# Joining the 64-token tails of two batches in the channel step of a fused attention and Wave-MLP kernel

## The chip, the cores and the metric

The kernel runs on one core of one Trainium2 chip. The metric is the device time of one execution in microseconds (us). A core has a matrix engine (TensorE, PE in the profile), a vector engine (VectorE, DVE), a scalar engine with function tables (ScalarE, ACT), a general engine (GpSimd, POOL) and a queue that issues transfers (SyncE, SP). Each takes its instructions in program order, and they wait for each other by semaphores.

## The reference, cut to what matters

There are 8 batches of 576 tokens, with 8 heads of 64 channels, all in float32. The first half is an attention with a pooled and a local part; its output `x` has 512 channels for each token. The second half mixes tokens and then channels:

```python
theta = x @ w_theta
zr, zi = x * cos(theta), x * sin(theta)
y = einsum('ts,bsd->btd', w_tok_r, zr) + einsum('ts,bsd->btd', w_tok_i, zi)
u = x + y
out = u + maximum(u @ w_ch, 0)
```

The change concerns `u` and the last line alone, and the order of the whole program.

## The kernel before

576 tokens are 4 chunks of 128 and a tail of 64. Everything is computed in steps of a few instructions, written as Python generators, one generator for each kind of step and all 8 batches one after the other. The string `ORDER` (line 80) has one letter for each step: `L` and `v` load q, k and v; `C` and `w` cast them (GpSimd mostly); `A` turns q and k so that channels lie on partitions (ScalarE copies the result, line 334; for batches 6 and 7 the turning itself is a DMA transpose, letter `q`, line 296); `Q`, `S` and `B` are pooled scores, band scores and pooled values; `N` and `V` are the two attention outputs (the third `N` step of a batch ends with a ScalarE copy, line 490); `T` transposes and adds them into `xT`; `H` makes the angles and their cosines and sines (lines 562 to 582); `Z` and `z` form z (lines 588 to 610); `X` mixes tokens (`mix`, lines 615 to 632); `u` turns `u` back with DMA transposes; `R` is the channel product (`channels`); `O` is the residual and the store (`store`). `l`, `c`, `h`, `g`, `W` are the weights, `D` is warm-up work for TensorE, `K` constants. A letter in the string takes the next step of its kind, so `X` letters 1 to 5 are batch 0. In the text "A7.2" means step 2 of the letter A for batch 7. A function `pin` ties each engine's instructions to just this order: the order in the string is the order on every engine and on the SP queue.

The accumulators have a fixed rotation too. Single-bank PSUM tiles come from `w1`, which goes round four tags, and two-bank tiles from `w2`, which goes round two. A step that takes a PSUM tile thus waits for whoever reads the tile of four (or two) allocations before.

For one batch the part that the change touches works so. `mix` makes `uT` (channels on partitions), 128 by 4 x 576: four chunks `dc` of 512 tokens (one `X` step each, nine matmuls of line 623) and the 64 tail tokens of all four in a fifth step (36 small matmuls, line 629). `u_turn` issues two DMA transposes on SP: `ur`, the 16 blocks of the main part (line 639), and `utr`, two blocks of the tail (line 641). `channels` has five steps: four chunks of 128 tokens, each of four matmuls of 512 columns (line 653), and the tail, for which the 64 tokens are put twice into the 128 columns of the array, each half giving 256 of the 512 channels: eight matmuls of 256 columns (line 661). `store` has five steps: one VectorE instruction each (`osb` = maximum(psr, 0) + ur, line 675), then one store of 128 tokens (line 681), and for the tail two stores of half the channels (line 684). `osb` has four buffers.

Of the kernel before, what the change touches and what calls it, by code (L numbers as in the profile page):

```python
# [10 lines left out]
BF16 = mybir.dt.bfloat16  # L11
AF = mybir.ActivationFunctionType
ALU = mybir.AluOpType
AX = mybir.AxisListType

P = 128
B = 8
H = 8
S = 576
# [22 lines left out]
HALF = 64  # L42
MAIN = 512
# [4 lines left out]
def kernel(  # L48
# [11 lines left out]
    nc = tc.nc  # L60
# [5 lines left out]
    moep = ctx.enter_context(tc.tile_pool(name="moep", bufs=2))  # L66
# [9 lines left out]
    def w1(name, dt=FP32):  # L76
        return ps1.tile([P, 512 if dt == FP32 else 1024], dt, tag="w1" + next(turn1), name=name)


    ORDER = (  # L80
        "LKLLLLLKKCLCCAvCCLvCDwvvvKLCAACwwwwLASCLSVQQCBlLLLLLVSlllllNvlCCCCNlvvvACNVCcScwcvTlTTccllcwAASlHVVH"
        "wwwDTTcAHZHZcHSZcccSDDhLLLzBcCSCWQDVWWLghLLLLCWCCvQvWWLNCNCCWWSWvvLvZNVVXwwwvAAvhwhTXTAALXSwSLLLLXQQ"
        "TBCCVgLggHCuLLVTvHNTVHHZNCCHCCCSwzZZZARRvvvSwOROALSXOLLAAXLLwSwwLvCCCCSCCCCRSNVOXVVXQVTTTAABwSXuTLLA"
        "vvwuvQRvvLLSTSHONNHVLLXuZZANHCLwHwwLVVHRQRRCCCCOzvLLLBOOCCSSTZTCvvRwOTLZSQHVHNVTXTAAXLLACACwCHHwCLCq"
        "LwwqNVHXSZNVXZZvvzSLLCCQCLqXVZLqQvRvwBvOVTVuTTLXTAwASSCHCCHCHNNXqvLwwTwuVXLVLAAHHXqSSZXRQROzONZSCCQC"
        "TCZBSVqROqvvvvZTSSROTVHVRHOTNNTXAAHVHHVwwwwwXAtAXSSzXXSSZZNZVuRuuRRROOQQtOOBRVRVttROtTTTOZOSTNXVRTuN"
        "RRxSSOOOHHVVXtttVHZHZZHNVzZXXttXuXTTXXHTHTTRxROOZHHRuROOHZRZZzOXXXXXXXRuRRRuuOORRuOOROROOORROO"
    )

    staged = {}  # L90
# [86 lines left out]
    for i in range(2):  # L177
        t = const.tile([P, 4, 5, KP], BF16, name=f"kdP{i}")
# [4 lines left out]
    for i in range(2):  # L183
        t = const.tile([P, 4, 5 * 120], BF16, name=f"kT{i}")
# [4 lines left out]
    for i in range(2):  # L189
        t = const.tile([P, NCH, H, 66], BF16, name=f"v_w{i}")  # L190
# [4 lines left out]
    for c in range(NCH):  # L195
        t = const.tile([P, DM], BF16, name=f"tmp{c}")
# [4 lines left out]
    for i in range(2):  # L201
        t = const.tile([P, 2, H, 66], BF16, name=f"vd{i}")
# [12 lines left out]
    wch = wpool.tile([P, 4, DM], BF16, name="wch")  # L215
# [305 lines left out]
    def parted(t):  # L521

        return (t[:, 0:4 * MAIN].rearrange("p (e t) -> p e t", e=4),
                t[:, 4 * MAIN:4 * S].rearrange("p (e t) -> p e t", e=4))
# [85 lines left out]
            yield  # L610


    uTs, urs = {}, {}

    def mix(b):

        (xA, xB), z = parted(xTs[b]), zs.pop(b)
        uT = uTs[b] = moep.tile([P, 4 * S], BF16, tag="uT", name=f"uT{b}")
        uA, uB = parted(uT)
        for dc in range(4):  # L620
            ps = w1(f"psu{dc}_{b}")
            for j in range(9):
                nc.tensor.matmul(out=ps, lhsT=z[:, j, P * dc:P * dc + P], rhs=WT[:, j, 0:MAIN], start=(j == 0), stop=(j == 8))  # L623
            nc.vector.tensor_tensor(out=uA[:, dc, :], in0=ps, in1=xA[:, dc, :], op=ALU.add)  # L624
            yield
        ps = w1(f"psut_{b}")[:, 0:4 * HALF].rearrange("p (e t) -> p e t", e=4)
        for dc in range(4):
            for j in range(9):
                nc.tensor.matmul(out=ps[:, dc, :], lhsT=z[:, j, P * dc:P * dc + P], rhs=WT[:, j, MAIN:S],  # L629
                                 start=(j == 0), stop=(j == 8))  # L630
        nc.vector.tensor_tensor(out=uB, in0=ps, in1=xB, op=ALU.add)
        yield

    def u_turn(b):

        ur = moep.tile([P, 16, P], BF16, tag="ur", name=f"ur{b}")
        utr = moep.tile([P, 2, P], BF16, tag="utr", name=f"utr{b}")
        urs[b] = ur, utr
        nc.sync.dma_start_transpose(out=ur, in_=uTs[b][:, 0:4 * MAIN])
        yield  # L640
        nc.sync.dma_start_transpose(out=utr, in_=uTs[b][:, 4 * MAIN:4 * S])
        yield

    rels = {}

    def channels(b):

        uA, uB = parted(uTs[b])
        for c in range(5):
            psr = rels[b, c] = w1(f"psr{c}_{b}")  # L650
            if c < 4:
                for dc in range(4):
                    nc.tensor.matmul(  # L653
                        out=psr, lhsT=uA[:, dc, P * c:P * c + P], rhs=wch[:, dc, :],
                        start=(dc == 0), stop=(dc == 3),
                    )
            else:

                for dc in range(4):
                    for hf in range(2):  # L660
                        nc.tensor.matmul(  # L661
                            out=psr[64 * hf:64 * hf + 64, 0:256], lhsT=uB[:, dc, :],
                            rhs=wch[:, dc, :].rearrange("p (j e d) -> p e j d", j=2, e=2)[:, hf],
                            start=(dc == 0), stop=(dc == 3),
                        )
            yield

    def store(b):

        ur, utr = urs.pop(b)  # L670
        for c in range(5):
            psr = rels.pop((b, c))
            osb = moep.tile([P, DM], FP32, tag="osb", bufs=4, name=f"osb{c}_{b}")
            n = 4 if c < 4 else 2
            nc.vector.scalar_tensor_tensor(  # L675
                out=osb[:, 0:P * n].rearrange("p (e d) -> p e d", d=P),
                in0=psr[:, 0:P * n].rearrange("p (e d) -> p e d", d=P), scalar=0.0,
                in1=ur[:, c:16:4, :] if c < 4 else utr, op0=ALU.max, op1=ALU.add,
            )
            if c < 4:  # L680
                nc.sync.dma_start(out=out[b, P * c:P * c + P, :], in_=osb)
            else:
                for hf in range(2):
                    nc.sync.dma_start(  # L684
                        out=out[b, 512:576, :].rearrange("t (j e d) -> e t j d", j=2, e=2)[hf],
                        in_=osb[64 * hf:64 * hf + 64, 0:2 * P].rearrange("p (j d) -> p j d", j=2),
                    )
            yield

    last = {}
# [13 lines left out]
    def batches(steps):  # L709
        for b in range(B):  # L710
            yield from steps(b)

    sequences = dict(L=batches(load), v=batches(load_v), C=batches(cast), w=batches(cast_v), A=batches(turns), B=batches(pooled_v), Q=batches(scores), S=batches(band_scores), N=batches(pooled_out), q=batches(turn_qk), t=batches(turn_x), x=batches(turn_z),
                     V=batches(outputs), T=batches(transposes), H=batches(phases), Z=batches(modulate),
                     K=constants(), z=batches(z_turn), u=batches(u_turn), X=batches(mix), R=batches(channels), O=batches(store),
                     l=weight_loads(), c=weight_casts(), h=channel_loads(), g=channel_casts(), W=weight_turns(), D=warm_up())
    pin()
# [35 lines left out]
```

## Time and profile before

| | before |
|---|---|
| time, median of 3 | 246.73 us (246.0 to 246.94) |
| profiled execution | span 247.0 us, 6608 instructions |
| TensorE busy | 224.8 us, 91% |
| VectorE busy | 184.6 us, 75% |
| ScalarE busy | 166.9 us, 68% |
| GpSimd busy | 160.9 us, 65% |
| tail of the channel product (line 661) | 64 matmuls, 5.0 us busy |
| tail of the residual (line 675, `utr`) | 8 instructions, 3.3 us |
| tail stores (line 684) | 16, of 64 KB each |
| `utr` transposes (line 641) | 8 |

The table is read together with where each piece stands. The busy time of TensorE is modelled for overlapping matmuls, so the start times of two successive instructions tell more about what one costs than its own duration does. An engine that is idle costs nothing as long as another one sets the pace.

### The profile page before, as it was taken

What the parts mean: (1) busy time and instruction counts of PE and PEld (TensorE: products, weight loads), DVE (VectorE), ACT (ScalarE), POOL (GpSimd) and SP (SyncE); (2) the same over time, 40 slices, a digit from 0 to 9 for tenths busy, and PEclk for the clock granted to TensorE, in tenths of its full rate; (3) what the DMA queues carried; (4) which work ended last, traced back from release to release, by engine and by line L of the source; (5) the groups of instructions that cost most, each with busy time, mean ns of one, the idle gap of its engine ahead of it and who ended that gap; (6) DMA issues with size and microseconds to landing.
All of it is one profiled execution on the core that took longest, in us unless ns stands there. A gap on an engine that the chain in (4) does not pass through costs nothing. (4 is left out here: it accounts for less than half of the span.)

```text
span 247.0 us, 6608 instructions
## 1 busy us (share of the span) xinstructions
PE 224.8 (91%) x2602; PEld 134.9 (55%) x2602; DVE 184.6 (75%) x345; ACT 166.9 (68%) x248; POOL 160.9 (65%) x223
## 2 busy tenths in 40 slices
PE   0778799999999999999999998999699999999990
PEld 0435465765566566656666555655455655455540
DVE  5274976679879898897989977997687776256462
ACT  3685799766998479988878999899924390250000
POOL 4467485997999999979759664996295942400000
PEclk9997999999999999999999999999989999999999
DMA  6999999999979997999999999599969594946496
GB/s 197 307 272 391 304 211 330 333 224 245 275 200 275 320 197 122 263 239 314 256 185 214 252 184 269 92 172 219 121 156 169 144 209 96 170 160 90 90 262 202
DMA packets 100511, 53.94 MB, mean 218 GB/s; under 512 B 83968, under 2 KB 86016, under 8 KB 100480
## 3 DMA queue, kind: packets, MB, share of 16 engines
q1 hardware_dynamic: 100480, 53.53, 93.3%
q8 instruction: 20, 0.33, 0.6%
q14 instruction: 11, 0.09, 0.2%
HBM read 33.59 MB, written 9.44 MB: 174 GB/s over the span
## 5 line engine op out<-in xcount | busy, mean ns | idle before, releaser
L623 PE MATMUL psu<-WT,z 128*128 128x512 bf16 x288 | 66.3, 379 | 0.5 <-ACT cs L568 0.5
L445 POOL TENSOR_SCALAR_AFFINE_SELECT pm<-pm 128x1024 bf16<-128x1024 bf16 (+1 forms) x35 | 36.6, 1045 | 20.0 <-ACT pm L438 20.0
L438 ACT ACTIVATE pm<-psS 128x1024 bf16<-128x1024 f32 (+1 forms) x40 | 37.7, 979 | 12.7 <-PE psS L430 11.9
L623 PEld LDWEIGHTS <-z 128*128 128x128 bf16 x288 | 26.8, 98 | 29.2 <-issue 0.8
L447 POOL TENSOR_SCALAR_AFFINE_SELECT pm<-pm 128x1024 bf16<-128x1024 bf16 (+1 forms) x35 | 36.6, 1045 | 2.4
L562 PE MATMUL psth<-wth,xT 128*128 128x512 bf16 x128 | 31.5, 379 | 0.1
L624 DVE TENSOR_TENSOR uT<-psu,xT 128x512 bf16<-128x512 f32 x32 | 21.8, 687 | 12.7 <-PE psu L623 12.6
L653 PE MATMUL psr<-wch,uT 128*128 128x512 bf16 x128 | 31.2, 383 | 0.0
L567 ACT ACTIVATE cs<-psth,pihc 128x512 bf16<-128x512 f32 x32 | 22.3, 697 | 11.8 <-PE psth L562 11.3
L131 POOL CAST v_w<-st_v 128x512 bf16<-128x512 f32 (+1 forms) x40 | 23.9, 614 | 9.2 <-DMA st_v<-in_v_dram 9.1
L511 DVE TENSOR_TENSOR tmp<-psloc,rl 120x512 bf16<-120x512 f32 (+2 forms) x40 | 27.6, 691 | 1.4
L342 DVE TENSOR_REDUCE qdT<-qT 128x288 bf16<-128x1152 bf16 x16 | 21.5, 1347 | 8.2 <-ACT qT L334 8.2
L675 DVE SCALAR_TENSOR_TENSOR osb<-psr,ur 128x512 f32<-128x512 f32 x32 | 21.6, 686 | 7.3 <-PE psr L653 6.7
L342 DVE TENSOR_REDUCE kdP<-kT 128x300 bf16<-128x1200 bf16 x16 | 22.3, 1397 | 5.8 <-ACT kT L334 5.8
L124 POOL CAST k_tm<-st_k 128x576 bf16<-128x576 f32 x32 | 21.5, 673 | 4.5 <-DMA st_k<-in_k_dram 4.3
L124 POOL CAST q_tm<-st_q 128x576 bf16<-128x576 f32 x28 | 18.7, 667 | 2.5 <-PE pstr L332 1.3
L334 ACT COPY qT<-pstr 128x576 bf16<-128x576 bf16 x24 | 14.2, 646 | 8.7 <-PE pstr L332 8.7
L545 DVE TENSOR_TENSOR xT<-xTps,xdT 128x480 bf16<-128x480 bf16 (+3 forms) x36 | 18.7, 548 | 0.9 <-PE xTps L541 0.7
L568 ACT ACTIVATE cs<-psth 128x512 bf16<-128x512 f32 x32 | 19.4, 606 | 0.0
L653 PEld LDWEIGHTS <-uT 128*128 128x128 bf16 x128 | 11.5, 99 | 12.2 <-issue 0.8
L430 PE MATMUL psS<-qT,kT 64*128 64x128 bf16 (+1 forms) x320 | 15.0, 220 | 3.1 <-ACT pm L438 2.2
L502 PEld LDWEIGHTS <-pm 128*128 128x128 bf16 (+1 forms) x320 | 14.9, 105 | 5.0 <-issue 0.7
(92 smaller groups left out, 390.2 us busy)
## 6 DMA issues: line engine op xcount, KB each, us to landing
st_q<-in_q_dram SPq DMA_DIRECT2D x32, 288.0 KB, 4.7
st_k<-in_k_dram SPq DMA_DIRECT2D x32, 288.0 KB, 5.0
st_v<-in_v_dram SPq DMA_DIRECT2D x32, 256.0 KB, 5.4
out_dram<-osb SPq DMA_DIRECT2D x32, 256.0 KB, 3.1
st_v<-in_v_dram SPq DMA_DIRECT2D x8, 192.0 KB, 4.8
tok<-in_moe_w_tok_r_dram SPq DMA_DIRECT2D x4, 288.0 KB, 7.6
tok<-in_moe_w_tok_i_dram SPq DMA_DIRECT2D x4, 288.0 KB, 4.2
th<-in_moe_w_theta_dram SPq DMA_DIRECT2D x2, 512.0 KB, 7.1
```

What stands on the lines that cost most here:

```text
L124: eng[i](out=dst[:, hh // 2, :, hh % 2, :], in_=staged.pop((b, f"{'qk'[i]}{hh}")).rearrange("p (r d) -> p r d", d=D))
L131: gp(out=v_ws[b % 2][0:KW[c], c, :, 0:D], in_=staged.pop((b, f"v{c}"))[0:KW[c], 0:DM].rearrange("p (h d) -> p h d", d=D))
L342: nc.vector.tensor_reduce(out=dst, in_=src, axis=AX.X, op=ALU.add)
L438: nc.scalar.activation(out=pv, in_=ps[0:kw].rearrange("p e (j w) -> p (e j) w", w=P)[:, :, 0:qn], func=AF.Exp, scale=SCL,)
L445: nc.gpsimd.affine_select(out=pv, in_=pv, compare_op=ALU.is_ge, fill=0.0, base=off, pattern=[[0, 8], [-1, qn]], channel_multiplier=1)
L447: nc.gpsimd.affine_select(out=pv, in_=pv, compare_op=ALU.is_ge, fill=0.0, base=6 - off, pattern=[[0, 8], [1, qn]], channel_multiplier=-1)
L511: nc.vector.tensor_tensor(out=tmp[0:cnt].rearrange("p (e j d) -> p e j d", e=2, j=4), in0=pv[0:cnt, :, :, 0:D], in1=rl[0:cnt].unsqueeze(3) ...
L562: nc.tensor.matmul(out=th, lhsT=xA[:, dc, P * c:P * c + P], rhs=wth[:, dc, :], start=(dc == 0), stop=(dc == 3),)
L567: nc.scalar.activation(out=cs[:, 0, :], in_=th, func=AF.Sin, bias=pihc, scale=1.0)
L623: nc.tensor.matmul(out=ps, lhsT=z[:, j, P * dc:P * dc + P], rhs=WT[:, j, 0:MAIN], start=(j == 0), stop=(j == 8))
L624: nc.vector.tensor_tensor(out=uA[:, dc, :], in0=ps, in1=xA[:, dc, :], op=ALU.add)
L653: nc.tensor.matmul(out=psr, lhsT=uA[:, dc, P * c:P * c + P], rhs=wch[:, dc, :], start=(dc == 0), stop=(dc == 3),)
```

## The change

The tails of batches 2i and 2i+1 become one chunk of 128 tokens. `u`'s tail gets a tile of its own, `uB`, for a pair of batches. The channel product, the residual and the store of the tails then happen once for a pair, in the steps of the odd batch, with the same form of instruction as any other chunk. The eight matmuls with the tail put twice into the array are gone, and so are the separate shapes in `store`. The purpose is fewer and more uniform instructions and transfers. Because even batches now have one `R`, `O` and `u` step fewer, the order string is a new one (682 letters for 694).

```diff
     def mix(b):
         (xA, xB), z = parted(xTs[b]), zs.pop(b)
-        uT = uTs[b] = moep.tile([P, 4 * S], BF16, tag="uT", name=f"uT{b}")
-        uA, uB = parted(uT)
+        uT = uTs[b] = moep.tile([P, 4 * MAIN], BF16, tag="uT", name=f"uT{b}")
+        uA = uT.rearrange("p (e t) -> p e t", e=4)
+        if b % 2 == 0:
+            uBs[b // 2] = moep.tile([P, 4, 2, HALF], BF16, tag="uB", name=f"uB{b // 2}")
+        uB = uBs[b // 2][:, :, b % 2, :]
...
     def u_turn(b):
-        nc.sync.dma_start_transpose(out=ur, in_=uTs[b][:, 0:4 * MAIN])
-        yield
-        nc.sync.dma_start_transpose(out=utr, in_=uTs[b][:, 4 * MAIN:4 * S])
-        yield
+        nc.sync.dma_start_transpose(out=ur, in_=uTs[b])
+        yield
+        if b % 2:
+            utr = utrs[b // 2] = moep.tile([P, 4, P], BF16, tag="utr", name=f"utr{b // 2}")
+            nc.sync.dma_start_transpose(out=utr, in_=uBs[b // 2].rearrange("p e i t -> p (e i t)"))
+            yield
...
     def channels(b):
-        for c in range(5):
+        for c in range(4 + b % 2):
             psr = rels[b, c] = w1(f"psr{c}_{b}")
-            if c < 4:
...
-            else:
-                for dc in range(4):
-                    for hf in range(2):
-                        nc.tensor.matmul(
-                            out=psr[64 * hf:64 * hf + 64, 0:256], lhsT=uB[:, dc, :],
-                            rhs=wch[:, dc, :].rearrange("p (j e d) -> p e j d", j=2, e=2)[:, hf],
-                            start=(dc == 0), stop=(dc == 3),
-                        )
+            for dc in range(4):
+                nc.tensor.matmul(
+                    out=psr, lhsT=uA[:, dc, P * c:P * c + P] if c < 4 else uBs[b // 2][:, dc],
+                    rhs=wch[:, dc, :], start=(dc == 0), stop=(dc == 3),
+                )
             yield
     def store(b):
-        for c in range(5):
+        for c in range(4 + b % 2):
...
             if c < 4:
                 nc.sync.dma_start(out=out[b, P * c:P * c + P, :], in_=osb)
             else:
-                for hf in range(2):
-                    nc.sync.dma_start(
-                        out=out[b, 512:576, :].rearrange("t (j e d) -> e t j d", j=2, e=2)[hf],
-                        in_=osb[64 * hf:64 * hf + 64, 0:2 * P].rearrange("p (j d) -> p j d", j=2),
-                    )
+                nc.sync.dma_start(out=out[b - 1:b + 1, 512:576, :], in_=osb)
             yield
```

Of the order, two stretches are spoken of later: from H5.0 to S7.1, and the end. In each the old order stands first.

```diff
-        H5.0 V5.4 R2.4 H5.1 O2.4 T5.3 N6.0 N6.1 T5.4 X4.0 A7.0 A7.1 H5.2 V6.0 H5.3 H5.4 V6.1
-        w7.0 w7.1 w7.2 w7.3 w7.4 X4.1 A7.2 t6.0 A7.3 X4.2 S6.3 S6.4 z5.0 X4.3 X4.4 S7.0 S7.1
+        H5.0 V5.4 H5.1 O2.3 v7.3 v7.4 N6.0 V6.0 T5.3 X4.0 T5.4 Z5.0 N6.1 A7.0 w7.2 A7.1 H5.2 H5.3 H5.4 V6.1
+        w7.3 w7.4 N6.2 A7.2 A7.3 X4.1 X4.2 S6.3 S6.4 X4.3 X4.4 S7.0 S7.1
...
-        X7.3 X7.4 R6.0 u6.0 R6.1 R6.2 R6.3 u6.1 u7.0 O6.0 O6.1 R6.4 R7.0 u7.1 O6.2 O6.3 R7.1 O6.4 R7.2 O7.0 O7.1 O7.2 R7.3 R7.4 O7.3 O7.4
+        X7.3 u6.0 u7.0 X7.4 R6.0 R6.1 R6.2 O6.0 O6.1 u7.1 R6.3 R7.0 O6.2 R7.1 R7.2 O6.3 O7.0 R7.3 R7.4 O7.1 O7.2 O7.3 O7.4
```

In the old order N6.2 came after S7.1.

More of the change, by code (lines that the diff above doesn't have):

```diff
@@ L80 @@
     ORDER = (
[L81 to L87, printed above, removed]
+        "LLLLLLKKCCCKKCLLvvvvCAvLDLLlCCLlllCwwAAASSSwwwVBCLvCQQVNNCAcCcCLlcNLLlllcTTCCvCcwASSHVVDTvvvccVTATww"
+        "AHllHZwwclHlZHSQDZzZDLLLLhcLLBSchQDccVWLLSWWWNCCCCCvNCCCWWSWWWvvvvvVVXwwvAANXAALwwXSwSTTLXLLQCQBggCL"
+        "LLTLHVVHTwVhThCNHHuwCCCZNHZAZZggCCSLLXzALLRSROONAvCvvLACCCXSwwSLwLLRSRCCCCvOVVvOXvvAVXAvvTBSSXQwLwww"
+        "VTTTATQSSHuNNZHXvCVwZANHHVVHLLLLRLLLQRRuzOOOCCCCCQBwTSSTTCCROvvSZHVVHZZNNXTLTAALLLXAAvLLCCHVHHCqwCwL"
+        "LqwwSXLvZNVXZSBVXzZvCCCLwLwCqLLQQqvvvTTTRuVVOXTAASSHXHTCNVXCCCLwCNwwAAHHqVHSNvXvvzXSLLQZZRqOZZSQRSBC"
+        "wCqCOVTROSwSTTqRVHVHOvvNVTXTZNAwAHHHVwwNAAXXSSXXSSZZZzRVuuuRRQQROOOBtStTOXVVtttRROTVTXTTxSSRHOOVVRRO"
+        "HtOttNNHHVZHNZZzZVXXXtTTXXtuTTXTHHHRHxRuOOROZROHRZZZzOXXXXXXuuXRRROOuRRORROORROOOO"
     )
@@ L610, in modulate @@
             yield
-    uTs, urs = {}, {}
+    uTs, uBs, urs, utrs = {}, {}, {}, {}
     def mix(b):
         (xA, xB), z = parted(xTs[b]), zs.pop(b)
-        uT = uTs[b] = moep.tile([P, 4 * S], BF16, tag="uT", name=f"uT{b}")
-        uA, uB = parted(uT)
+        uT = uTs[b] = moep.tile([P, 4 * MAIN], BF16, tag="uT", name=f"uT{b}")
[3 more added lines that the diff above has]
+        uB = uBs[b // 2][:, :, b % 2, :]
         for dc in range(4):
@@ L634, in u_turn @@
     def u_turn(b):
-        ur = moep.tile([P, 16, P], BF16, tag="ur", name=f"ur{b}")
-        utr = moep.tile([P, 2, P], BF16, tag="utr", name=f"utr{b}")
-        urs[b] = ur, utr
-        nc.sync.dma_start_transpose(out=ur, in_=uTs[b][:, 0:4 * MAIN])
+        ur = urs[b] = moep.tile([P, 16, P], BF16, tag="ur", name=f"ur{b}")
+        nc.sync.dma_start_transpose(out=ur, in_=uTs[b])
         yield
-        nc.sync.dma_start_transpose(out=utr, in_=uTs[b][:, 4 * MAIN:4 * S])
-        yield
+        if b % 2:
+            utr = utrs[b // 2] = moep.tile([P, 4, P], BF16, tag="utr", name=f"utr{b // 2}")
+            nc.sync.dma_start_transpose(out=utr, in_=uBs[b // 2].rearrange("p e i t -> p (e i t)"))
+            yield
@@ L644 @@
     rels = {}
     def channels(b):
-        uA, uB = parted(uTs[b])
-        for c in range(5):
+        uA = uTs[b].rearrange("p (e t) -> p e t", e=4)
+        for c in range(4 + b % 2):
             psr = rels[b, c] = w1(f"psr{c}_{b}")
-            if c < 4:
-                for dc in range(4):
-                    nc.tensor.matmul(
-                        out=psr, lhsT=uA[:, dc, P * c:P * c + P], rhs=wch[:, dc, :],
-                        start=(dc == 0), stop=(dc == 3),
-                    )
-            else:
-                for dc in range(4):
-                    for hf in range(2):
-                        nc.tensor.matmul(
-                            out=psr[64 * hf:64 * hf + 64, 0:256], lhsT=uB[:, dc, :],
-                            rhs=wch[:, dc, :].rearrange("p (j e d) -> p e j d", j=2, e=2)[:, hf],
-                            start=(dc == 0), stop=(dc == 3),
-                        )
+            for dc in range(4):
[3 more added lines that the diff above has]
+                )
@@ L666, in channels @@
             yield
     def store(b):
-        ur, utr = urs.pop(b)
-        for c in range(5):
+        ur = urs.pop(b)
+        for c in range(4 + b % 2):
             psr = rels.pop((b, c))
             osb = moep.tile([P, DM], FP32, tag="osb", bufs=4, name=f"osb{c}_{b}")
-            n = 4 if c < 4 else 2
             nc.vector.scalar_tensor_tensor(
-                out=osb[:, 0:P * n].rearrange("p (e d) -> p e d", d=P),
-                in0=psr[:, 0:P * n].rearrange("p (e d) -> p e d", d=P), scalar=0.0,
-                in1=ur[:, c:16:4, :] if c < 4 else utr, op0=ALU.max, op1=ALU.add,
+                out=osb.rearrange("p (e d) -> p e d", d=P),
+                in0=psr.rearrange("p (e d) -> p e d", d=P), scalar=0.0,
+                in1=ur[:, c:16:4, :] if c < 4 else utrs.pop(b // 2), op0=ALU.max, op1=ALU.add,
@@ L682, in store @@
             else:
-                for hf in range(2):
-                    nc.sync.dma_start(
-                        out=out[b, 512:576, :].rearrange("t (j e d) -> e t j d", j=2, e=2)[hf],
-                        in_=osb[64 * hf:64 * hf + 64, 0:2 * P].rearrange("p (j d) -> p j d", j=2),
-                    )
+                nc.sync.dma_start(out=out[b - 1:b + 1, 512:576, :], in_=osb)
             yield
```

## The prediction

> **What bounds the kernel now.** I read the busy shares first, then a table of busy time by stretch, then the timelines of TensorE, ScalarE and the SP queue where that table shows a change of limit.
>
> ```profile
> PE 224.8 (91%) x2602; PEld 134.9 (55%) x2602; DVE 184.6 (75%) x345; ACT 166.9 (68%) x248; POOL 160.9 (65%) x223
> ...
> 138.56:159.91 21.35, 19.96 (x265) 12.10 (x264) 17.46 (x32) 20.09 (x27) 15.64 (x21) 1.00 1.05 195
> 159.91:177.38 17.47, 15.52 (x176) 9.14 (x174) 14.29 (x25) 17.43 (x22) 10.85 (x14) 1.00 1.00 168
> 177.38:207.49 30.11, 29.84 (x332) 17.74 (x332) 22.97 (x45) 14.81 (x23) 20.06 (x22) 0.94 0.75 158
> 207.49:233.34 25.85, 25.85 (x207) 13.24 (x204) 12.13 (x20) 5.23 (x10) 4.81 (x6) 1.00 0.67 128
> 233.34:241.50 8.16, 8.12 (x48) 3.57 (x46) 5.52 (x9) 0.00 (x0) 0.00 (x0) 1.00 0.84 220
> 241.50:247.00 5.50, 0.00 (x0) 0.00 (x0) 1.20 (x3) 0.00 (x0) 0.00 (x0) 0.95 0.63 212
> ```
>
> After the length come TensorE, its weight loads, VectorE, ScalarE and GpSimd, then the granted clock. TensorE is the bound over all; but from 138.56 to 177.38 ScalarE is busy 37.5 of 38.8 us, and TensorE waits for it. From 177.38 to 241.5 TensorE is full. The last 5.5 us have no TensorE work: they are residuals and stores. What TensorE saves counts before 138 and after 177; what it saves between is lost in its wait.
>
> ```profile
> 172.63 2.36 ACT L334 COPY kT<-qk 128x576 bf16<-128x576 bf16 x2
> 175.01 1.28 ACT L438 ACT_TABLE_LOAD   x1
> 176.30 3.52 ACT L438 ACTIVATE pm<-psS 128x1024 bf16<-128x1024 f32 x4
> ```
>
> ```profile
> 174.25 1.21 PE L629 MATMUL psut<-WT,z 128*128 128x64 bf16 x36
> 177.38 0.40 PE L430 MATMUL psS<-qT,kT 64*128 64x128 bf16 x8 [1.92 <-ACT pm L438]
> 178.04 0.55 PE L430 MATMUL psS<-qT,kT 64*128 64x128 bf16 x8 [0.27 <-ACT pm L438]
> ```
>
> ```profile
> 174.90:178.30 3.40, 1.22 (x36) 1.04 (x31) 2.93 (x4) 3.37 (x5) 0.91 (x1) 0.98 0.62 136
> 178.30:181.70 3.40, 3.40 (x37) 2.62 (x33) 2.45 (x5) 2.16 (x3) 3.26 (x5) 0.52 0.83 154
> ```
>
> S7.0 needs the two-bank accumulator that the exponential of S6.3 reads, and that stands behind A7.3 and a table load. TensorE waits 1.92 and 0.27 us, and the next 3.4 us run at a clock of 0.52. With TensorE full there, that costs 3.4 x 0.48 = 1.6 us more.
>
> ```profile
> 220.23 0.63 PE L574 MATMUL pstt<-xT,wth 128*128 128x64 bf16 x16
> 220.79 0.63 PE L661 MATMUL psr<-wch,uT 128*64 128x256 bf16 x8
> 221.35 2.12 PE L623 MATMUL psu<-WT,z 128*128 128x512 bf16 x9
> ```
>
> The old tail's eight matmuls take 0.56 us from start to start; the sixteen before them take 0.47 in the chain of waits and start at 220.23, so 220.70 was due and they begin 0.1 us late. One old tail costs TensorE 0.66 us. A chunk of four 512-column matmuls takes 0.86 to 0.87 us (the 16 of 233.17 need 3.45).
>
> ```profile
> 240.84 0.63 PE L661 MATMUL psr<-wch,uT 128*64 128x256 bf16 x8
> 241.96 0.69 DVE L675 SCALAR_TENSOR_TENSOR osb<-psr,ur 128x512 f32<-128x512 f32 x1 [0.38 <-DMA out_dram<-osb]
> 242.79 0.42 DVE L675 SCALAR_TENSOR_TENSOR osb<-psr,utr 128x256 f32<-128x256 f32 x1
> 243.24 1.19 SPq L684 DMA_DIRECT2D out_dram<-osb  x2
> ```
>
> At the end VectorE waits for `osb` buffers, freed by stores; then two tail stores are issued, one after the other.
>
> [...] a store is 0.33 to 0.6 us on SP and 2 to 3.6 us to landing. [...]
>
> **The change part by part.**
>
> *Channel product.* A pair now costs 0.86 us where it cost 2 x 0.66 = 1.32. By place: R0.4 goes and R1.4 gets longer, before 138: -0.46. R2.4 stood inside the ScalarE-bound stretch (at 160.1), so its removal is absorbed; R3.4 comes after and costs +0.20. R4.4 and R5.4: -0.46. The last pair is counted with the end. Sum -0.72 us.
>
> *Residual, transposes, stores.* VectorE loses 2 x 0.42 and gains 0.69 for a pair: 0.15 us, hidden, as VectorE is under 60% after 207 and TensorE is the bound earlier. SP loses for a pair one transpose (1.19 us) and three of four tail store issues (0.59 each): 3.0 us, 12 in all. Before the end this is hidden: GpSimd waits for loads almost only before 40 us. For a tail transpose of four blocks I use z's row, also four blocks: 1.2 us on SP, 3.3 to landing, between utr's 2.8 and ur's 5.3. It hides behind nine chunks of product.
>
> *Waits added.* The tail of an even batch waits for the odd one: no engine stands still for it, as the steps are simply later in the order. The last utr transpose is issued after O6.1, and O6.2's store queues behind it on SP for 1.2 us, as it did before.
>
> *Order, ScalarE.* From H5.0 to S7.0 the ScalarE chain was table 1.28, H5.0 and H5.1 2.3, A7.0 and A7.1 4.5, the rest of H5 3.2, A7.2 and A7.3 4.5, table 1.28, one exponential 1.03. The new order puts N6.2 into it, with a copy of 0.65 us (line 490) that used to run at 180. TensorE reaches S7.1 0.65 us later: +0.65.
>
> *Order, accumulators.* Without R2.4, but with Z5.0 and N6.2 moved forward, the single-bank rotation shifts: X4.1 now needs the tile that H5.2's sines read. Counted from H5.0, TensorE is at X4.1 after 8.6 us (4 chunk products 3.5, X4.0 1.94, the rest small), and ScalarE ends H5.2 at about 10.0. So TensorE waits 1.4 us at X4.1 and 17.5 to 19.15, 1.65 us, at S7.0: the idle time is split and the later wait is shorter. The wait at X4.1 lies under the ScalarE chain and costs nothing by itself. If no window is then as empty as the 1.22 of 3.40 above, the half-rate window is not triggered where TensorE is full: -1.6 to -1.7 us.
>
> *End.* Let T0 be the end of X7.4 (233.33 before). Before, the product ended at T0+8.14 and the kernel at T0+13.67. Now nine chunks of 0.865 end at T0+7.8. O6.0 is at T0+0.9 and its store lands at about T0+5.2 (3.57 us, as in the chain); O7.0 takes its buffer and runs to about T0+6.5; its store lands at about T0+9.0; O7.4 takes that buffer, 9.0 to 9.7; one store instead of two (issue 0.5, landing 2.3 to 2.8) ends at about T0+12.7. That is -0.96 us, last pair included. If stores land 1 us sooner or later the end is T0+11.9 to 13.7.
>
> Sum: 246.73 - 0.72 + 0.65 - 0.96 - 1.7 = 244.0 us.
>
> **Rivals.**
>
> *The half-rate window stays.* All as above, but the wait at S7.0 still leaves a window too empty, or the one at X4.1 does. For it: 1.65 us plus a second short wait is about half a window. [...] 245.7 us, which is within 0.5%.
>
> *The new order opens waits in full stretches; slower.* From 42 to 138 TensorE has hardly a gap, and the new string changes all of that. z0.0 now stands before all of L2 on SP: its data come at about 39 us, so L2.0 goes at about 40.5 instead of 36.5, and lands at about 45 with C2.0 wanted near 46.5. T6.0 stands behind S7.2's two selections (2.2 us) on GpSimd, and H6.0 waits for it. Two such waits of 1.5 us with the half-rate window kept give 245.7 + 3.0 = 248.7, slower. Against it: TensorE's work, summed from its rows up to each of X1.0 to X6.0, differs by 1.3 us at most between the orders, but for X5.0, which has 4 us less ahead of it.
>
> *The front gets shorter.* H0.0 comes before A1.2 and A1.3; their loads go later. H0.0 could start near 26.5 instead of 29.8 us. But W needs all weight loads, which the transfers (share about 1 in the first 50 us) finish near 40 us in either order, so at most 1.5 us arrive at X0.0: 242.5.
>
> **How the numbers follow.** Forecast 244.0: 0.42. Window stays, 245.7: 0.28. Waits opened, 248.7: 0.17. Front shorter, 242.5: 0.13. Faster by over 0.5% is below 245.5: the forecast, the front, and a small part of the second case, less some of the forecast for small waits: 0.58. Slower, above 247.96: 0.17. The rest, 0.25, is the same. The range runs from 241.9 (front case, end 0.6 sooner) to 248.0, which leaves out most of the slower case.
>
> **What would show it.** Line 661 gone and 16 more matmuls of line 653; four utr transposes and four tail stores; the last product about 7.8 us after X7.4 and the end about 5 us after that. Near S7.0: the ScalarE chain with a copy of line 490 before A7.2, a TensorE wait of about 1.4 us at an X4 step and of 1.65 at S7.0, and no stretch near 0.5 of the clock after 170 us. The forecast is wrong if that stretch stands, or if TensorE starts X0.0 much later than 50.35 us or has new waits before 138 or after 180.

## The result, and the profile after

The changed kernel takes 255.95 us (254.36 to 256.55) where the kernel before takes 246.83; the ratio is 1.036, with an interval of 1.0301 to 1.0418. It is slower by 3.6%, where 244.0 us had been forecast. The profiled execution has a span of 254.8 us.

The page shows that TensorE has less to do, as meant, and a smaller share:

```profile
PE 221.1 (87%) x2517; PEld 134.6 (53%) x2554; DVE 186.6 (73%) x341; ACT 167.1 (66%) x248; POOL 161.7 (63%) x223
```

Read from the end. These are the last pieces of work in the changed kernel's timeline:

```profile
241.10 1.34 DVE L667 SCALAR_TENSOR_TENSOR osb<-psr,ur 128x512 f32<-128x512 f32 x2 [1.46 <-DMA out_dram<-osb]
241.98 0.75 PEld L655 LDWEIGHTS <-uB 128*128 128x128 bf16 x4
242.19 1.03 PE L655 MATMUL psr<-wch,uB 128*128 128x512 bf16 x4
243.30 1.40 DVE L667 SCALAR_TENSOR_TENSOR osb<-psr,ur 128x512 f32<-128x512 f32 x2 [0.86 <-PE psr L655]
244.69 0.69 DVE L667 SCALAR_TENSOR_TENSOR osb<-psr,utr 128x512 f32<-128x512 f32 x1
245.41 0.54 SPq L675 DMA_DIRECT2D out_dram<-osb  x1
```

The last store (line 675, 256 KB, the tails of batches 6 and 7) is issued at 245.41, and the span ends at 254.8. For 9.4 us no engine has work, and the program waits for its stores. In the kernel before, 3.8 us passed from 243.24 to the end, with two stores to issue. What the store does is seen in a table of stretches after it; the last two columns are the busy share of the 16 DMA engines and GB/s:

```profile
247.50:249.50 2.00, 0.00 (x0) 0.00 (x0) 0.00 (x0) 0.00 (x0) 0.00 (x0) 0.50 0.13 32
249.50:251.50 2.00, 0.00 (x0) 0.00 (x0) 0.00 (x0) 0.00 (x0) 0.00 (x0) 0.50 0.13 50
251.50:253.50 2.00, 0.00 (x0) 0.00 (x0) 0.00 (x0) 0.00 (x0) 0.00 (x0) 0.50 0.09 35
```

A share of 0.13 is what 2 of 16 engines give when they are busy all the time (0.125), and the rate is 32 to 50 GB/s. The packets of the trace say the same. The 128 packets of 2 KB of this store run from 246.58 to 252.93; two are under way at once for 5.8 us of this time, and never more than three. A group of two packets of 4 bytes (252.92 and 252.93) closes it, where sixteen (246.25 to 246.39) close the store of 128 tokens just before it. So this store is carried, by its share and its packets, by two engines.

The same store of batches 2 and 3 does harm in the middle. Three views of the changed kernel: its chain of waits, the VectorE timeline, the TensorE timeline.

```profile
191.80 8.00 DMA out_dram<-osb
```

```profile
195.36 0.68 DVE L667 SCALAR_TENSOR_TENSOR osb<-psr,ur 128x512 f32<-128x512 f32 x1
199.89 0.69 DVE L667 SCALAR_TENSOR_TENSOR osb<-psr,ur 128x512 f32<-128x512 f32 x1 [3.85 <-DMA out_dram<-osb]
```

```profile
201.56 0.47 PE L502 MATMUL psloc<-v_w,pm 128*128 128x65 bf16 x8 [2.34 <-DVE rd L476]
```

The store, issued at 191.80, takes 8.0 us to land and holds its `osb` buffer until then. The residual that takes this buffer next stands still for 3.85 us, and with it everything behind it on VectorE. TensorE needs one of these results and waits 2.34 us. Then its clock falls to 0.59 (the column before the DMA share):

```profile
199.00:202.40 3.40, 1.06 (x21) 0.88 (x20) 2.41 (x7) 1.69 (x4) 0.00 (x0) 0.91 0.98 284
202.40:205.80 3.40, 3.33 (x31) 2.21 (x30) 3.26 (x6) 1.28 (x3) 0.00 (x0) 0.59 0.95 227
```

The stretch before S7.0, on which the forecast turned, looks as it was drawn there. First the TensorE timeline, then ScalarE's, then stretches:

```profile
168.60 4.04 PE L626 MATMUL psu<-WT,z 128*128 128x512 bf16 x17 [1.43 <-ACT cs L568]
...
177.50 0.40 PE L430 MATMUL psS<-qT,kT 64*128 64x128 bf16 x8 [1.25 <-ACT pm L438]
178.17 0.40 PE L430 MATMUL psS<-qT,kT 64*128 64x128 bf16 x8 [0.27 <-ACT pm L438]
```

```profile
170.10 0.67 ACT L490 COPY xdT<-psxd 128x576 bf16<-128x576 bf16 x1
```

```profile
174.30:177.70 3.40, 2.15 (x49) 1.67 (x47) 2.58 (x5) 3.37 (x4) 0.18 (x1) 1.00 0.71 134
177.70:181.10 3.40, 3.08 (x43) 2.01 (x39) 3.10 (x8) 2.25 (x3) 3.26 (x4) 1.00 0.51 95
```

The wait is split over two places, the copy of N6.2 (line 490) stands in ScalarE's chain, and the clock stays at 1.00.

### The profile page after: what moved, and what is told of

It reads as the page before. It is cut to its first block, busy times and chain, and to the rows that moved or that the text cites. A ratio compares the mean times of both kernels' runs of the same rounds, so it can differ in the third digit from the quotient of the medians.

```text
span 254.8 us, 6438 instructions
## 1 busy us (share of the span) xinstructions
PE 221.1 (87%) x2517; PEld 134.6 (53%) x2554; DVE 186.6 (73%) x341; ACT 167.1 (66%) x248; POOL 161.7 (63%) x223
## 4 chain that ended last, share of the span: by engine, by line
PE 52%; ACT 14%; POOL 11%; DMA 8%; DVE 7%; issue 4%; SPq 1%; DVEq 0%; ACTq 0%; POOLq 0%
PE psu L626 19%; PE psr L655 7%; PE psth L562 5%; DMA out_dram<-osb 4%; POOL pm L445 4%; DMA st_q<-in_q_dram 4%; PE pstr L332 3%; POOL pm L447 3%; PE psloc L502 3%; ACT kT L334 3%; ACT pm L438 3%; PE psS L430 3%; DVE tmp L511 2%; DVE osb L667 2%; PE xTps L541 2%
## 5 line engine op out<-in xcount | busy, mean ns | idle before, releaser
L562 PE MATMUL psth<-wth,xT 128*128 128x512 bf16 x116 | 30.3, 379 | 0.9 <-issue 0.3
L655 PE MATMUL psr<-wch,uT 128*128 128x512 bf16 x118 | 30.3, 380 | 0.6 <-issue 0.2
L568 ACT ACTIVATE cs<-psth 128x512 bf16<-128x512 f32 x32 | 19.4, 606 | 0.0
L502 PE MATMUL psloc<-v_w,pm 128*128 128x65 bf16 (+1 forms) x320 | 16.5, 198 | 3.2 <-DVE rd L476 2.3
L605 DVE TENSOR_TENSOR z<-psxt,cs 128x1024 bf16<-128x1024 bf16 x24 | 15.8, 683 | 2.6 <-PE psxt L604 2.1
```

The costliest lines, as they stand in the source:

```text
L502: nc.tensor.matmul(out=pv[0:qn, h // 4, h % 4, :], lhsT=pms[b][c][0:kw, 4 * par + blk, 0:qn], rhs=v_w[0:kw, c, h, 0:65], start=(h % 4 == 0 ...
L562: nc.tensor.matmul(out=th, lhsT=xA[:, dc, P * c:P * c + P], rhs=wth[:, dc, :], start=(dc == 0), stop=(dc == 3),)
L655: nc.tensor.matmul(out=psr, lhsT=uA[:, dc, P * c:P * c + P] if c < 4 else uBs[b // 2][:, dc], rhs=wch[:, dc, :], start=(dc == 0), stop=(dc ...
```

## The experiments

Theory S: the view of `out` that the new store writes begins with a dimension of 2, so two engines carry it. Rival O: the new order. Rival Q: transfers that wait in the queue ahead of the store, or one large store as such. Each ratio is to the kernel before on the same chip.

**Two stores for a pair, new order.**

```diff
-                nc.sync.dma_start(out=out[b - 1:b + 1, 512:576, :], in_=osb)
+                for i in range(2):
+                    nc.sync.dma_start(out=out[b - 1 + i, 512:576, :], in_=osb[64 * i:64 * i + 64, :])
```

> The changed kernel, but the tail store of a pair goes as two stores of 64 tokens each. Theory S (the store): the changed kernel's one store, whose output view begins with a dimension of 2, is carried by few of the 16 DMA engines and so takes 8 to 9 us to land; it costs about 6 us at the end (the last store is issued at 245.4 and the span ends at 254.8, where 2.3 to 2.8 us to landing were due) and, by holding an osb buffer, 2.3 us of TensorE wait at 199 with a half-rate window after it of 1.7 us. Two stores land in 2 to 3 us each: 255.9 - 6 - 4 = 245.5 to 246.5 us. Rival O (the new order is at fault): 253 us or more, since the order is unchanged. Rival Q (transfers queue up: transposes before the store hold it): 254 to 256.

Measured: 246.48 us, ratio 0.9942 (0.9909 to 0.9976), span 246.0. The loss is gone, and the change is now a small gain. Rivals O and Q (in its queue form) fall.

**The old order with the change in it.** The order string is the old one without R, O and u steps for the tails of even batches.

> The change with the order of the kernel before, of which only the letters of the steps that are gone (tail steps of even batches) are struck out; the store as in the changed kernel. Theory S: the end is long as in the changed kernel, so at least 246.8 - 1.5 + 6 = 251.5 us; up to 256 if a slow store also holds an osb buffer in the middle. Rival O: 245.5 to 246.5. Rival Q: the late transposes are at the same places as before, so about 247.

Measured: 255.79 us, ratio 1.0304 (1.0249 to 1.0358). Theory S allowed up to 256 if the store also does harm in the middle. It does, but by another way than the `osb` buffer. The order has a transpose (line 304) right behind the store of batches 2 and 3 on SP. GpSimd waits 3.70 us for that transpose, its masks come late, and TensorE waits 1.97 us for them. In the next run, with the same order and two stores, TensorE has no such wait from 180 us on. In the GpSimd and TensorE timelines:

```profile
198.67 0.95 POOL L545 TENSOR_TENSOR xT<-xt,xdT 128x112 bf16<-128x112 bf16 x2 [3.70 <-DMA xt<-tmp]
```

```profile
201.89 0.43 PE L502 MATMUL psloc<-v_w,pm 128*128 128x65 bf16 x8 [1.97 <-POOL pm L447]
```

Rival O expected 246.

**The old order, two stores.** Both edits above.

> As the run with the old order, and the pair's tail store in two. This is the change without its new order and without its one store. Theory S and rival O: 245 to 246.5 us. What it differs from the two-store run with the new order is what the new order is worth: by my working the front gains 1.5 us (X0.0 at 48.85 instead of 50.35) and loses it again in waits on ScalarE before 178, so no more than 1 us either way.

Measured: 247.39 us, ratio 0.999 (0.9956 to 1.0024). The change in the code alone, with quick stores, is worth nothing that can be measured in the old order. The new order with quick stores gives 0.9942, thus about 0.5% from the order, though the two intervals overlap a little.

**One store, the tokens of two batches interleaved.** The bytes and the number of stores are those of the changed kernel; the first dimension of the view is 64 instead of 2. The transpose and the matmul read `uB` in its new order; these two lines are left out here.

```diff
-            uBs[b // 2] = moep.tile([P, 4, 2, HALF], BF16, tag="uB", name=f"uB{b // 2}")
-        uB = uBs[b // 2][:, :, b % 2, :]
+            uBs[b // 2] = moep.tile([P, 4, HALF, 2], BF16, tag="uB", name=f"uB{b // 2}")
+        uB = uBs[b // 2][:, :, :, b % 2]
...
-                nc.sync.dma_start(out=out[b - 1:b + 1, 512:576, :], in_=osb)
+                nc.sync.dma_start(out=out[b - 1:b + 1, 512:576, :].rearrange("i t d -> t i d"), in_=osb)
```

> The changed kernel with one store for a pair as it has, of the same 256 KB, but the two batches' tail tokens interleaved on the partitions (token 0 of both, token 1 of both), so that the output view begins with a dimension of 64 instead of 2. Nothing is left out. Theory S in the form that the first dimension sets how many engines carry the store: the store lands in 2 to 3 us and the time is that of the two-store run within 0.7 us, 245 to 246.5. If merging into one 256 KB store is itself slow (rival Q, or one large store to two distant places): 254 to 256 as in the changed kernel.

Measured: 246.15 us, ratio 0.9911 (0.9887 to 0.9936), span 244.7. The end of its SP timeline, and a stretch after the last issue:

```profile
240.68 0.57 SPq L675 DMA_DIRECT2D out_dram<-osb  x1
```

```profile
241.50:242.50 1.00, 0.00 (x0) 0.00 (x0) 0.00 (x0) 0.00 (x0) 0.00 (x0) 1.00 0.64 240
```

The share is 0.64 at 240 GB/s, and 4.0 us pass from issue to the end of the span instead of 9.4. The size of the store and its two distant targets are not what was slow.

**Two stores for a pair, split by channels.** Each still begins with a dimension of 2.

```diff
-                nc.sync.dma_start(out=out[b - 1:b + 1, 512:576, :], in_=osb)
+                for i in range(2):
+                    nc.sync.dma_start(out=out[b - 1:b + 1, 512:576, 256 * i:256 * i + 256], in_=osb[:, 256 * i:256 * i + 256])
```

> The changed kernel with two stores for a pair as in the two-store run, but split by channels: each has both batches' 64 tokens and 256 channels, so the output view of each still begins with a dimension of 2. Theory S, in which that first dimension sets the number of engines: still slow, two stores of 128 packets of 1 KB on the same two engines: 253 to 258 us. Rival (what helped was having two smaller stores): 245.5 to 247.

Measured: 254.85 us, ratio 1.029 (1.0227 to 1.0352). Half the size and twice the number do not help; two stretches after the last issue show about the same share as in the changed kernel (0.13):

```profile
247.00:249.00 2.00, 0.00 (x0) 0.00 (x0) 0.00 (x0) 0.00 (x0) 0.00 (x0) 0.50 0.14 42
249.00:251.00 2.00, 0.00 (x0) 0.00 (x0) 0.00 (x0) 0.00 (x0) 0.00 (x0) 0.50 0.14 48
```

**Only the last pair's store in two.** The edit of the first experiment under `if b == 7`.

> The changed kernel; only the store of the last pair (batches 6 and 7) goes in two, the other three pairs keep the one store. Theory S: the end shrinks by about 6 us, the wait at 199 stays: 255.9 - 6 = 249.5 to 250.5 us. A rival in which only the end matters: 246 to 247. A rival in which the middle matters more: 252 or more.

Measured: 250.97 us, ratio 1.0136 (1.0059 to 1.0214). By the ratios 2.2%, about 5.5 us, came from the end, near the 6 expected. The wait in the middle stands, in its TensorE timeline:

```profile
200.91 0.41 PE L502 MATMUL psloc<-v_w,pm 128*128 128x65 bf16 x8 [2.62 <-DVE rd L476]
```

**Only the store of batches 2 and 3 in two.** The same under `if b == 3`.

> The changed kernel; only the store of batches 2 and 3 (issued at 191.8 us in the changed kernel) goes in two. Theory S: the VectorE wait of 3.85 us for an osb buffer at 196 to 199.9 and the TensorE wait of 2.34 us go, and the half-rate window that followed goes in most executions: 251.5 to 253.5 us, the end as long as before (8 to 9 us after the last store). Rival (that wait came from the 5.2 us transpose ahead on the same queue): no change, 255 to 256.

Measured: 252.3 us, ratio 1.0199 (1.0127 to 1.0271). The stretch from 180 to 210 us has no wait and a full clock (third column from the right):

```profile
180.00:210.00 30.00, 29.63 (x288) 16.16 (x292) 21.23 (x42) 11.85 (x19) 21.47 (x25) 1.00 0.81 170
```

With the last pair split alone, TensorE was busy 26.84 us of this stretch, at a clock of 0.94. The rival that this run was to test blamed a transpose of 5.2 us that follows the store on SP. That transpose is itself an effect of the store: with this one store in two, it takes 1.84 us. The changed kernel's line stands first.

```profile
194.46 5.21 SPq L312 DMA_TRANSPOSE xr<-xT  x1
```

```profile
194.06 1.84 SPq L312 DMA_TRANSPOSE xr<-xT  x1
```

By ratios the middle is worth 1.036 - 1.020 = 1.6% and the end 2.2%, each uncertain by about 0.9%; all four stores together are worth 4.2%.

**N6.2 back behind S7.1, in the interleaved kernel.** One letter of the order string is moved.

```diff
-        V6.1 w7.3 w7.4 N6.2 A7.2 A7.3 X4.1 X4.2 S6.3 S6.4 X4.3 X4.4 S7.0 S7.1
+        V6.1 w7.3 w7.4 A7.2 A7.3 X4.1 X4.2 S6.3 S6.4 X4.3 X4.4 S7.0 S7.1 N6.2
```

> The kernel with interleaved tails (246.15 us, ratio 0.991), with one letter moved: N6.2, which the new order put ahead of A7.2, goes back behind S7.1. It tests the two steps of the prediction on the stretch before S7.0. Theory C (clock): without N6.2 ahead, X4.1 takes an accumulator that is free, so TensorE reaches S7.0 early and waits once, about 1.9 to 2.2 us, and a half-rate window after it comes back in most executions: S7.1 about 0.65 us earlier, but 1.6 us lost after it, so about 1 us slower, 246.8 to 247.5. Rival L (the ScalarE chain alone matters): 0.65 us faster, 245.3 to 245.7.

Measured: 249.18 us, ratio 1.0056 (1.0022 to 1.009). The interleaved kernel, on other chips, had 0.9911 and in a later measurement 0.9952, so this is 1.0 to 1.5% slower. The direction is that of theory C. The size, 2.5 to 3.6 us, is larger than its 1 us, and what makes up the rest stays open. In its TensorE timeline the wait is one again, and the row of granted clock on its page has a dip after it, in the slice that begins at 179.0 us (the 30th digit):

```profile
177.40 0.40 PE L430 MATMUL psS<-qT,kT 64*128 64x128 bf16 x8 [1.92 <-ACT pm L438]
```

```profile
PEclk9997999999999999999999999999979999999996
```

S7.1 did not come earlier, as it was expected to. But this execution was already late before the letter that was moved: ScalarE's chain, which begins with the table load ahead of H5.0, began 0.73 us later. The table load and S7.1, in the profile of the interleaved kernel and then here:

```profile
159.20 1.28 ACT L567 ACT_TABLE_LOAD   x1 [0.76 <-issue]
...
177.84 0.40 PE L430 MATMUL psS<-qT,kT 64*128 64x128 bf16 x8 [0.27 <-ACT pm L438]
```

```profile
159.93 1.28 ACT L567 ACT_TABLE_LOAD   x1 [0.76 <-issue]
...
178.07 0.47 PE L430 MATMUL psS<-qT,kT 64*128 64x128 bf16 x8 [0.27 <-ACT pm L438]
```

From the one to the other it is 18.64 us in the interleaved kernel and 18.14 here. The chain is 0.50 us shorter without N6.2, near the 0.65 of the expectation.

**N6.2 ahead of A7.2, in the kernel before.** Again one letter.

```diff
-        V6.1 w7.0 w7.1 w7.2 w7.3 w7.4 X4.1 A7.2 t6.0 A7.3 X4.2 S6.3 S6.4 z5.0 X4.3 X4.4 S7.0 S7.1
+        V6.1 N6.2 w7.0 w7.1 w7.2 w7.3 w7.4 X4.1 A7.2 t6.0 A7.3 X4.2 S6.3 S6.4 z5.0 X4.3 X4.4 S7.0 S7.1
```

> The kernel before, with one letter moved: N6.2 from behind S7.1 to behind V6.1, ahead of A7.2, as in the new order. Theory C: ScalarE's chain gets 0.65 us longer, but the idle time of TensorE is split between X4.1 (1.4 us) and S7.0 (1 to 1.3), and the half-rate window after S7.1 goes away: 0.65 - 1.65 = 1 us faster than before, ratio 0.995 to 0.997. Rival L: 0.65 us slower, ratio 1.002 to 1.004. Rival F (the window falls by chance): no difference on the mean, mean granted clocks spread alike in both.

Measured: 246.79 us where the kernel before had 247.59; ratio 0.9968 (0.9951 to 0.9986), as theory C had it. From its TensorE timeline and stretches:

```profile
168.49 4.05 PE L623 MATMUL psu<-WT,z 128*128 128x512 bf16 x17 [0.95 <-ACT cs L568]
...
177.39 0.40 PE L430 MATMUL psS<-qT,kT 64*128 64x128 bf16 x8 [1.26 <-ACT pm L438]
```

```profile
174.90:178.30 3.40, 1.88 (x53) 1.66 (x51) 2.93 (x4) 3.37 (x5) 0.89 (x1) 1.00 0.46 101
178.30:181.70 3.40, 3.35 (x36) 2.02 (x32) 2.84 (x6) 1.53 (x2) 3.26 (x5) 1.00 0.83 154
```

S7.0 starts where it did in the kernel before (177.38), but the clock after it is 1.00 and not 0.52. Rival F (chance) falls too. None of the 22 executions of this kernel had a mean granted clock below 0.987, where 12 of 36 of the kernel before did; and all 15 executions with N6.2 moved back in the interleaved kernel were at 0.987 or below. The profiled executions of the two kernels agree: from 177 to 184 us the kernel before, with N6.2 behind S7.1, has a mean clock of 0.76, and the changed kernel, with N6.2 ahead of A7.2, has 1.00.

**Six `osb` buffers, and the interleaved kernel once more beside it.**

```diff
-            osb = moep.tile([P, DM], FP32, tag="osb", bufs=4, name=f"osb{c}_{b}")
+            osb = moep.tile([P, DM], FP32, tag="osb", bufs=6, name=f"osb{c}_{b}")
```

> The kernel with interleaved tails, and six osb buffers instead of four. It tests the step on the end: there O7.0 to O7.3 wait for osb buffers (1.23 and 0.86 us) that come free only when a store has landed. If that chain sets the last residual, O7.4 ends about 0.8 us after the last matmul group instead of 1.9, and the kernel is 0.8 to 1.2 us faster than the interleaved kernel of the same call. Rival (the store queue or the transposes set it: ur of batch 7 lands late): no change within 0.3 us.

> The kernel with interleaved tails once more, on the same chip as the run with six osb buffers, for the comparison and a narrower interval: 0.989 to 0.994 of the kernel before, as it was.

Measured: six buffers 246.07 us, ratio 0.9924 (0.9901 to 0.9947); four buffers 246.77 us, 0.9952 (0.9931 to 0.9973). On VectorE at the end of the run with six:

```profile
236.82 2.04 DVE L667 SCALAR_TENSOR_TENSOR osb<-psr,ur 128x512 f32<-128x512 f32 x3 [0.55 <-DMA ur<-uT]
239.03 0.69 DVE L667 SCALAR_TENSOR_TENSOR osb<-psr,ur 128x512 f32<-128x512 f32 x1 [0.17 <-PE psr L655]
239.90 0.69 DVE L667 SCALAR_TENSOR_TENSOR osb<-psr,utr 128x512 f32<-128x512 f32 x1 [0.17 <-PE psr L655]
```

The waits for buffers are gone; what is left is one for `ur` of batch 7 and then TensorE's own pace. The last residual ends at 240.59, 0.9 us after the last matmul group (238.83 + 0.86), where it was 2.05 us in the run beside it (242.81 against 239.90 + 0.86). The gain of 0.7 us on the median is a little below the expected 0.8 to 1.2, and the two intervals overlap; the shorter wait in the trace is clearer than the time. This version, new order, interleaved tails and six buffers, is faster than both kernels.

## Why the prediction was wrong

**The step that failed** is the last term of *End*: "one store instead of two (issue 0.5, landing 2.3 to 2.8)". The landing was taken from stores of another shape. Issue and landing together measured 9.4 us to the end of the span, and 8.0 us for the store at 191.80. T0, the end of X7.4, follows from the last tail step of `mix`, in the changed kernel and then in the interleaved one:

```profile
234.24 1.21 PE L632 MATMUL psut<-WT,z 128*128 128x64 bf16 x36
```

```profile
229.81 1.21 PE L632 MATMUL psut<-WT,z 128*128 128x64 bf16 x36
```

In the changed kernel T0 is 235.45. The last residual was done at T0+9.9, near the 9.7 of the forecast, but the end came at T0+19.4 instead of T0+12.7. So *End* was wrong by 6.6 us, and nearly all of it is this store.

The same price was left out once more in *Residual, transposes, stores*, where the tail store counted only for the SP time that it saves and was called hidden before the end. That its buffer and the transfers behind it on SP would wait for it was put at nothing. The second rival, at 0.17, did stand for a slower kernel with new waits. One came after 180 us, but from a store, which it did not name; its time of 248.7 and the range up to 248.0 lay far too low as well. The prediction's "2 to 3.6 us to landing" was also too narrow for the kernel before: there the stores of line 681 took 2.0 to 6.2 us (median 3.1) and those of line 684 2.1 to 4.6 (median 2.8).

The runs show the cause from three sides: the same store with another first dimension is quick (0.9911), smaller stores with the first dimension 2 are slow (1.029), and in both slow forms a share of 0.13 to 0.14 of the DMA engines is busy. The traces show it at both ends: a share of 0.13 and two closing packets for the view that begins with 2, a share of 0.64 for the one that begins with 64, and sixteen closing packets for the store of 128 tokens, whose view begins with 128. Values between 2 and 64 were not tried, so how the share follows from the view is not shown.

**What the failed step cost** was 4.2%: about 2.2% at the end, about 1.6% in the middle through the `osb` buffer, with the half-rate window after it, and a rest of 0.4%, within the noise, with the other two stores or the overlap of the parts.

**What held.** *Channel product*: from T0 = 235.45 the product ends at 242.19 + 1.03, T0+7.8, as forecast. *Order, ScalarE*: the copy of line 490 is in the chain. From the table load ahead of H5.0 to S7.1 it was 18.13 us in the kernel before (159.91 to 178.04) and is 18.65 (159.52 to 178.17), so 0.5 us longer where 0.65 was forecast. *Order, accumulators*: 1.4 us was forecast at X4.1 and 1.43 measured; at S7.0 1.65 and 1.25. *The half-rate window*: gone there in the profile of the changed kernel (the one at 202 us comes from the slow store: with that store in two, the clock was 1.00 from 180 to 210 us), and moving one letter takes it away in the kernel before (a clock of 1.00 for 0.52, ratio 0.9968) and brings one back in the interleaved kernel (a digit of 7 in the clock row at 179.0 us, ratio 1.0056), so it is measured and not only argued that the window comes and goes with the place of N6.2. What in the idle time brings it is not shown. *Front*: X0.0 began at 48.85 us, not 50.35, so the third rival's first half came true; it was used up by S7.1, where both kernels are level.

**What was mis-sized.** With the store mended, the interleaved kernel has a span of 244.7 us and ratios of 0.991 and 0.995 in two measurements, where the forecast stood for 0.989. A part of the missing gain is the end: its T0 is 231.02, thus 2.3 us earlier than before, but the kernel ends 13.7 us after it, just as before, and not 12.7. The last residual was done at T0+9.6, as forecast; the quick store of 256 KB needs 4.0 us from issue to end instead of about 3. So one store in place of two saved nothing at the end. The change without its order and with two stores measures 0.999 (0.9956 to 1.0024). The 0.72 us of *Channel product* and the 0.96 of *End* together, 0.7%, lie outside that interval, so they did not both arrive in that order; 0.72 alone would fit it.

## What to carry to other kernels

Merging two transfers into one was not free here: with a view that begins with 2, 9.4 us passed from the issue of the last store to the end, at a DMA share of 0.13; with one that begins with 64 and has the same 256 KB it was 4.0 us, at 0.64. So look at how the merged view begins, or at the DMA share while it alone is in flight, before pricing it by rows of another shape. The slow store hurt at the end of the program (about 2.2%) and also in the middle (about 1.6%): through the buffer that it held for 8.0 us, for which VectorE stood still for 3.85 us with everything behind it, and in the old order through the transfer behind it in its queue, for which GpSimd waited 3.70 us. And a wait of TensorE had a second price, the clock after it: a wait of 1.92 us before S7.0 was followed by a clock of 0.52, and waits of 0.95 and 1.26 us, at X4.1 and S7.0, by 1.00. The two short waits were cheaper than the long one (0.9968), though ScalarE's chain was 0.5 us longer with N6.2 in it.

## What the runs showed of the hardware

The half-rate window is not the same in every execution. Over 36 executions of the kernel before on one chip, with mean granted clocks from 0.979 to 0.999, the median was 248.8 us for the 7 below 0.983, 247.7 for the 19 between 0.983 and 0.995, and 246.6 for the 10 from 0.995 on. From the first group to the last, whose middle clocks are 0.979 and 0.998, that is about 0.8 us for each step of 0.007. Such a step is one window of 3.41 us at half rate in 247 us, as the clock of the kernel before has it from 178.16 to 181.57. So one window more or less is near a third of the 2.7 us that the change was forecast to bring. The mean does not tell which window it was: the profiled execution of the kernel before has one near the start as well as the one after S7.0.

How little work of TensorE brings such a window did not come out as one number. Near S7.0, a stretch of 3.40 us with 1.22 us of TensorE work was followed by a clock of 0.52, and ones with 1.88 and 2.15 us were not. But near the start of the kernel before a stretch with 2.25 us was:

```profile
14.30:17.70 3.40, 2.25 (x34) 1.17 (x32) 3.14 (x4) 2.62 (x4) 2.03 (x4) 1.00 1.07 293
17.70:21.10 3.40, 3.40 (x43) 1.58 (x42) 0.90 (x2) 2.18 (x5) 2.40 (x5) 0.50 1.03 386
```

The busy time of TensorE is modelled, so it is not a measure by which to set a limit.
